# A recurrence, a soft mixture of experts and a dense layer: the range check of the decays moved from the recurrence to the dense stage

## The chip, the cores and the metric

The kernel runs on 1 core of one Trainium2 chip. The metric is device time in microseconds (us) of one execution. Engines: PE multiplies matrices (PEld loads its weights), ACT applies functions and copies, DVE does vector work, POOL does side work, SP issues the transfers (DMA).

## The reference

Three layers follow each other. The first is a recurrence over 768 tokens for 4 batches of 8 heads, the second mixes the tokens softly into 32 slots of 8 experts and back, the third is a dense layer with a sigmoid GELU.

```
for t in range(S):                                  # recurrence
    y[:, :, t] = r_t . (state + (u * k_t) v_t^T)
    state = w_t * state + k_t v_t^T
logits = x @ phi                                    # mixture
slot_input = softmax(logits, 0).T @ x
slot_out[e] = relu(slot_input[e] @ w1[e]) @ w2[e]
x = softmax(logits, 1) @ slot_out
h = x @ w_in                                        # dense layer
out = (h * sigmoid(1.702 * h)) @ w_out
```

The decays w lie between 0.80 and 0.95. The kernel's fast way of doing the recurrence holds only for decays in a range, so it checks them, and falls back to a general way where the check fails. With these inputs it never does.

## The kernel before, in words

**Recurrence** (`phase_a`). 16 pairs of heads are worked on in a software pipeline, one round of the loop `for i in range(n_p + 1)` for each. In round i DVE scans the decays of pair i+1 forward and backward (`products`, L489 to L493), masks the two halves of the scores of pair i (`causal`, L564), scans the states (`states`, L548), scales keys and queries (`scale`, L499) and turns coefficients (`coef_tr`, L523). ACT writes diagonals (`diagonal`, L530, six small ones for each half), copies transposed keys (`keys_tr`, L539), decays (L505), outputs (L583) and their transposes (L597). A mask needs the diagonal of its half. PE makes scores, states, outputs and transposes. SP issues in program order: decays z of pair i+2, then, once PE has finished the outputs of pair i-1, the keys and queries of pair i+3, the values v of pair i+1, and pieces of later weights.

**The check.** `checks` (L510) runs two exponentials over the 1550 decays of two pairs on ACT, summing them into `stat`: in round 0, and at the end of each odd round. They stand ahead of the next round's work on ACT, and read both buffers of z.

**Mixture, end** (`phase_b`). PE applies first weights (L983), then for experts 0 to 7 the second (L1010, 8 products each). Meanwhile DVE converts `w_in` from 64-bit floats in steps (`in_step`, L289 to L302, with ACT's L297 between). After expert 4, `in_range` compares `stat` and the decay products on DVE (L313, L315, L317), sums the flags over the partitions with a one-column product on PE (L319) and copies the sum into `flag` (L320).

**Dense stage** (`phase_c`). A prologue scales and folds the experts' result (L1061 on ACT, L1065 on PE, L1067 on DVE), makes the layer's table (L1073), repeats it over the partitions (L1085), places it, and starts the pipeline: `act` (L1096), GELU (L1103), a high and a low part (L1110 ACT, L1118 DVE). Between these stand steps that convert `w_out` (`step`, the same L289 to L302). Then come 96 steps of nine products each (`project`, L1134), one for each of 6 blocks of 512 tokens and 16 column blocks. Every finished block is added up on DVE (L1154) and stored by SP (L1155).

All of this stands in an order written by hand, and every engine takes its own instructions in that order. `keep_warm` (L279) issues products whose result nobody reads.

Of the kernel before, what the change touches and what calls it, by code (L numbers as in the profile page):

```python
# [7 lines left out]
F32 = mybir.dt.float32  # L8
# [11 lines left out]
NP = H // 2  # L20
# [18 lines left out]
NFLAG = 128 * (1 + NC) * B * NP  # L39
PMIN = 1e-15  # L40
# [166 lines left out]
def body(ctx, tc, rkz, z0, vin, vt, uin, phi, w1, w2, w_in, w_out, cst, out):  # L207
# [10 lines left out]
    stat = cpool.tile([128, 2, B * NP // 2], F32, name="stat")  # L218
# [3 lines left out]
    ubias = cpool.tile([128, 1], F32, name="ubias")  # L222
    soft = [con, ident, phis, tokens, SI, negm, Zs]

    def consts():
        nc.sync.dma_start(out=u_sb, in_=uin)
        nc.sync.dma_start(out=con, in_=cst)
        nc.sync.dma_start(out=phis, in_=phi)
        nc.gpsimd.memset(ebias, -916.0 * 2.0 ** 23)
        nc.gpsimd.memset(ubias, -52.0)  # L230

    with ExitStack() as c1:
        wip = c1.enter_context(tc.tile_pool(name="wip", bufs=1, reuse_waits="tile"))
        ring = c1.enter_context(tc.tile_pool(name="ring", bufs=1, reuse_waits="tile"))
        with tc.manual_schedule(), ExitStack() as c2:
            W = Weights(tc, ring, wip, w1, w2, w_in, w_out)
            short = ExitStack()
            batches, sp, sT, in_step = phase_a(tc, rkz, z0, vin, u_sb, stat, prod, ebias, ubias, W, c2, short, consts, soft)
            dense = phase_b(tc, W, c2, short, sp, sT, soft, batches,
                            lambda room, ps: in_range(tc, stat, prod, con, flag, room, ps), in_step)  # L240
            phase_c(tc, W, c2, dense, ebias, soft, out)
# [65 lines left out]
def in_range(tc, stat, prod, con, flag, room, ps):  # L307

    nc = tc.nc
    m = B * NP  # L310
    g = room[:, 0:NFLAG // 128]
    n = room[:, NFLAG // 128:NFLAG // 128 + 1]
    nc.vector.tensor_scalar(out=g[:, 0:m], in0=stat.rearrange("p a n -> p (a n)"), scalar1=2 * NC + 2.5, scalar2=None,  # L313
                            op0=ALU.is_le)
    nc.vector.tensor_scalar(out=g[:, m:], in0=prod.rearrange("p a n -> p (a n)"), scalar1=PMIN, scalar2=None,  # L315
                            op0=ALU.is_gt)
    nc.vector.tensor_reduce(out=n, in_=g, axis=AX.X, op=ALU.add)  # L317
    pf = ps.tile([128, 512], F32, name="ps")
    nc.tensor.matmul(pf[0:1, 0:1], n, con[:, OFF_SGN:OFF_SGN + 1], start=True, stop=True)  # L319
    nc.vector.tensor_copy(flag, pf[0:1, 0:1])  # L320
# [87 lines left out]
def phase_a(tc, rkz, z0, vin, u_sb, stat, prod, ebias, ubias, W, after, late, consts, soft):  # L408
# [5 lines left out]
    with ExitStack() as ctx:  # L414
# [12 lines left out]
        zz = s0[:, 0:2 * ZW]  # L427
        dX = s0[:, 2 * ZW:2 * ZW + XL]
        half = s0[:, 2 * ZW + XL:].bitcast(BF16)
        dS, junk = half[:, 0:XL], half[:, XL:XL + ZW]  # L430
# [75 lines left out]

        def checks(p):

            for i, (sc, bi) in enumerate(((-30.0, 0.0), (40.0, ubias))):
                nc.scalar.activation(junk.bitcast(mybir.dt.uint8), zz, AF.Exp, scale=sc, bias=bi, accum_out=stat[:, i, p // 2:p // 2 + 1])  # L510
# [134 lines left out]
        for i in range(n_p + 1):  # L645
# [7 lines left out]
            load_z(i + 2)  # L653
            if cur:
                keys_tr(i)
            if cur and i:
                diagonal(i, 0)
# [66 lines left out]
            if i % 2 and nxt or i == 0:  # L724
                checks(i + 1 if i else 0)
# [205 lines left out]
def phase_b(tc, W, after, late, sp, sT, soft, batches=(), check=None, in_step=lambda: None):  # L931
# [6 lines left out]
    with late:  # L938
# [68 lines left out]
        for e in range(NE):  # L1007
# [14 lines left out]
            if check and e == 4:  # L1022
                check(room(), psS)
# [6 lines left out]
def phase_c(tc, W, after, dense, ebias, soft, out):  # L1030
# [3 lines left out]
    with ExitStack() as c2:  # L1034
# [133 lines left out]
        step(0, 1)  # L1168
        for kt in range(KT):
            scaled(kt)  # L1170
        folded()
        pm = psA.tile([128, 512], F32, name="pa")
# [4 lines left out]
        prs = [psS.tile([128, 512], F32, name="ps"), psR.tile([128, 512], F32, name="ps")]  # L1177
        for q in range(2):
            repeat(0, q, prs[q])
        step(0, 3)  # L1180
# [4 lines left out]
        act(1)  # L1185
        gelu(0)
# [27 lines left out]
        going = [[step, 2, 3, 5], [step, 3, 1, 5]]  # L1214
# [82 lines left out]
```

## Time and profile before

| | |
|---|---|
| time, 3 runs | 454.34 us median (453.66 to 455.0) |
| profiled execution | 453.75 us, of which the span of its instructions is 452.0 us |
| busy: PE, DVE, ACT | 403.9, 316.7, 280.5 us |
| recurrence, from the first scan to the end of the last pair | about 0 to 180 us |
| end of the mixture, prologue of the dense stage | about 180 to 222 us |
| 96 dense steps | 222 to 446 us, on PE almost without a gap |

A stretch is read in the rows further down by its busy time on each engine (PE, PEld, DVE, ACT, POOL, each with its instructions in brackets), then the clock granted to PE (1.00 is 2.4 GHz, 0.50 is 1.2 GHz), the mean busy share of the 16 DMA engines, and GB/s. A row of the timeline gives start and length in us, engine, line, operation, operands, and in brackets how long the engine sat idle ahead of it and what ended that. A row of waits gives the total, the number of times and the longest.

### The profile page before, as it was taken

How to read it: one execution, taken by the hardware profiler on the slowest of the kernel's cores; microseconds unless marked ns; L12 is line 12 of the kernel's file. 1: busy time of each engine (PE TensorE's matmuls, PEld its weight loads, DVE VectorE, ACT ScalarE, POOL GpSimd, SP SyncE). 2: the span in 40 equal slices, each digit the busy share in tenths (PEclk: the TensorE clock that was granted, in tenths of full speed). 3: DMA queues.
4: the chain of work that ended last, by engine and by line, in shares of the span. 5: the costliest groups of instructions: out<-in, count | busy, mean ns of one | idle time of the engine just before them, and what ended most of it. 6: DMA issues, size and time to landing. Idle time of an engine off the chain costs nothing.

```text
span 452.0 us, 8818 instructions
## 1 busy us (share of the span) xinstructions
PE 403.9 (89%) x3390; PEld 306.3 (68%) x3392; DVE 316.7 (70%) x529; ACT 280.5 (62%) x630; POOL 47.6 (11%) x81
## 2 busy tenths in 40 slices
PE   4888888978888779986799999999999999999994
PEld 1566666656666657362588878878788888888883
DVE  7898898889889975664897597776775424424332
ACT  4788878788787856231687475665756444444440
POOL 4322222222222102200000000000000000000000
PEclk9699999999999889996899999999999999999999
DMA  8969899797684568999900000000000101101012
GB/s 200 214 195 280 258 232 270 204 265 220 163 216 126 167 274 296 394 413 347 369 0 1 0 2 0 1 1 0 1 1 0 71 1 71 70 0 71 22 48 78
DMA packets 21107, 62.60 MB, mean 139 GB/s; under 512 B 2464, under 2 KB 3104, under 8 KB 20800
## 3 DMA queue, kind: packets, MB, share of 16 engines
q1 hardware_dynamic: 21056, 61.95, 44.1%
q8 instruction: 28, 0.46, 0.4%
q14 instruction: 23, 0.19, 0.1%
HBM read 57.23 MB, written 4.72 MB: 137 GB/s over the span
## 4 chain that ended last, share of the span: by engine, by line
PE 64%; DVE 13%; ACT 13%; DMA 5%; issue 3%; POOL 1%; DVEq 0%; SPq 0%; ACTq 0%; POOLq 0%
PE po L1134 43%; ACT wt L510 5%; DMA wt<-in_rkz 5%; PE pa L1096 5%; ACT am L530 4%; PE ps L983 2%; PE py L575 2%; PE py L580 2%; DVE wt L499 2%; PE ps L1010 2%; PE pg L558 2%; DVE am L564 1%; ACT cT L539 1%; DVE wt L489 1%; DVE st L548 1%
## 5 line engine op out<-in xcount | busy, mean ns | idle before, releaser
L1118 DVE TENSOR_TENSOR gl<-g,gh 128x512 fp32r<-128x512 f32 x96 | 65.1, 688 | 57.9 <-ACT gh L1110 57.5
L1110 ACT CAST gh<-g 128x512 fp32r<-128x512 f32 x96 | 59.4, 619 | 62.4 <-PE po L1134 62.0
L1134 PE MATMUL po<-gh,wi 128*128 128x512 f32 x288 | 88.6, 389 | 0.0
L1134 PE MATMUL po<-gh,wt 128*128 128x512 f32 x288 | 84.8, 395 | 0.0
L1134 PEld LDWEIGHTS po<-gh,wt 128*128 128x128 f32 x288 | 55.0, 191 | 12.2 <-issue 0.4
L530 ACT ACTIVATE am<-con,cT 128x128 f32<-128x128 f32 x192 | 59.6, 396 | 4.9 <-DVE cT L523 4.9
L1134 PEld LDWEIGHTS po<-gh,wi 128*128 128x128 f32 x288 | 54.2, 188 | 11.6
L1103 ACT ACTIVATE g<-pa 128x512 f32<-128x512 f32 x96 | 57.1, 595 | 2.8 <-PE pa L1096 2.8
L1134 PE MATMUL po<-gl,wi 128*128 128x512 f32 x144 | 56.3, 391 | 0.0
L1134 PE MATMUL po<-gl,wt 128*128 128x512 f32 x144 | 51.4, 393 | 1.4 <-DVE gl L1118 1.4
L564 DVE COPY_PREDICATED am<-con,pg 128x768 f32<-128x768 uint32 x32 | 32.4, 1011 | 14.4 <-ACT am L530 14.4
L1096 PE MATMUL pa<-cT,wt 128*128 128x512 f32 x96 | 38.5, 403 | 1.8 <-ACT g L1103 1.6
L558 PE MATMUL pg<-wt 64*128 64x128 f32 x312 | 26.6, 307 | 7.7 <-DVE am L564 7.7
L1134 PEld LDWEIGHTS po<-gl,wt 128*128 128x128 f32 x144 | 27.2, 189 | 8.0 <-DVE gl L1118 2.2
L1134 PEld LDWEIGHTS po<-gl,wi 128*128 128x128 f32 x144 | 27.0, 188 | 5.6
L558 PEld LDWEIGHTS pg<-wt 64*128 64x128 f32 x312 | 21.3, 203 | 13.4 <-DVE am L564 9.7
L489 DVE TENSOR_TENSOR_SCAN wt<-wt 128x774 f32<-128x774 f32 (+1 forms) x17 | 28.1, 1661 | 1.0 <-DMA wt<-in_rkz 0.7
L493 DVE TENSOR_TENSOR_SCAN wt<-wt 128x774 f32<-128x774 f32 x16 | 28.4, 1772 | 0.5
L575 PE MATMUL py<-am,v 128*64 128x128 f32 x384 | 28.4, 284 | 0.0
L483 POOL TENSOR_TENSOR rkb<-wt 128x384 f32<-128x384 f32 x25 | 26.4, 1056 | 14.0 <-DMA wt<-in_rkz 9.5
L596 PE MATMUL ps<-con,xt 128*128 128x128 f32 x96 | 16.4, 284 | 8.7 <-DVE cT L523 4.8
L583 ACT COPY xt<-py 128x384 f32<-128x384 f32 x32 | 14.7, 478 | 13.3 <-PE py L580 13.3
(208 smaller groups left out, 579.9 us busy)
## 6 DMA issues: line engine op xcount, KB each, us to landing
wt<-in_w SPq DMA_DIRECT2D x21, 512.0 KB, 6.8
wt<-in_w SPq DMA_DIRECT2D x13, 768.0 KB, 7.2
wt<-in_rkz SPq DMA_DIRECT2D x26, 288.0 KB, 4.9
v<-in_vin SPq DMA_DIRECT2D x16, 296.0 KB, 5.2
out_dram<-os SPq DMA_DIRECT2D x18, 256.0 KB, 2.1
wt<-in_rkz SPq DMA_DIRECT2D x30, 145.3 KB, 6.3
wi<-in_w_in SPq DMA_DIRECT2D x6, 512.0 KB, 5.8
w2t<-in_w SPq DMA_DIRECT2D x4, 768.0 KB, 7.7
```

The costliest lines, as they stand in the source:

```text
L483: eng.tensor_tensor(out=rkb[:, c], in0=st[p]["r"][:, c], in1=st[p]["k"][:, c], op=ALU.mult)
L489: nc.vector.tensor_tensor_scan(out=sf[:, o:n][:, ::-1], data0=z[:, o + 1:n + 1][:, ::-1], data1=dS[:, o:n][:, ::-1], initial=0.0, op0=ALU. ...
L493: nc.vector.tensor_tensor_scan(out=x, data0=z[:, 0:XL], data1=dX, initial=0.0, op0=ALU.mult, op1=ALU.add)
L530: nc.scalar.activation(am[:, j, c], ident, AF.Copy, scale=q["coef"][:, c0 + c, j:j + 1])
L558: nc.tensor.matmul(q["pg"][:, j, (c - c0) * CH:(c - c0 + 1) * CH], q["k"][64 * j:64 * j + 64, c * CH:(c + 1) * CH], q["r"][64 * j:64 * j + ...
L564: nc.vector.copy_predicated(q["am", c0], later, q["pg"][:, :, 0:3 * CH].rearrange("p j (c t) -> p j c t", t=CH))
L575: nc.tensor.matmul(py[64 * j:64 * j + 64, (c - c0) * CH:(c - c0 + 1) * CH], q["v"][:, c * 96 + j * 48:c * 96 + j * 48 + 64], q["am", c0][: ...
L1096: nc.tensor.matmul(pa, mst[:, f * 128:(f + 1) * 128], cT.at(tb * 512, 512), start=True, stop=True)
L1103: nc.scalar.activation(g, live[n], AF.Gelu_apprx_sigmoid)
L1110: nc.scalar.copy(gh, live[n])
L1118: nc.vector.tensor_tensor(out=gl, in0=g, in1=gh.bitcast(F32), op=ALU.subtract)
L1134: nc.tensor.matmul(live["po", tb][i], w[:, i * 128:(i + 1) * 128], g, start=(f % FH == 0 and k == 0), stop=(f % FH == FH - 1 and k == 2))
```

## The change

The two exponentials are gone from the recurrence, with `stat` and their scratch room. ACT's first half of diagonals moves ahead of the copies of keys. In the dense stage the decays are read a second time, as 24 pieces of 128x384 numbers (196.6 KB each) into three rotating rooms, and DVE takes the largest absolute value of each, two steps after its load. The flags are summed in step 90 of 96. The prologue gets 17 idle products in five places.

```
 class Check:
     def load(self, i, room):
         self.t[i] = room
         self.tc.nc.sync.dma_start(out=room, in_=self.wc[:, i * (NW // NCK):(i + 1) * (NW // NCK)])
     def part(self, i):
         self.tc.nc.vector.tensor_reduce(out=self.peak[:, i:i + 1], in_=self.t.pop(i), axis=AX.X, op=ALU.max,
                                         apply_absolute_value=True)
     def result(self, room, pf):
         nc = self.tc.nc
         g, n = room[:, 0:NFLAG // 128], room[:, NFLAG // 128:NFLAG // 128 + 1]
         nc.vector.tensor_scalar(out=g[:, 0:NCK], in0=self.peak, scalar1=WMAX, scalar2=None, op0=ALU.is_le)
         ...
         nc.vector.tensor_reduce(out=n, in_=g, axis=AX.X, op=ALU.add)
         nc.tensor.matmul(pf[0:1, 0:1], n, self.con[:, OFF_SGN:OFF_SGN + 1], start=True, stop=True)
         nc.vector.tensor_copy(self.flag, pf[0:1, 0:1])
@@ phase_a
-        def checks(p):
-            for i, (sc, bi) in enumerate(((-30.0, 0.0), (40.0, ubias))):
-                nc.scalar.activation(junk.bitcast(mybir.dt.uint8), zz, AF.Exp, scale=sc, bias=bi, accum_out=stat[:, i, p // 2:p // 2 + 1])
...
+            if cur and i:
+                diagonal(i, 0)
             if cur:
                 keys_tr(i)
-            if cur and i:
-                diagonal(i, 0)
...
-            if i % 2 and nxt or i == 0:
-                checks(i + 1 if i else 0)
@@ phase_b
-            if check and e == 4:
-                check(room(), psS)
@@ phase_c
+        idle = con[:, 0:320].bitcast(BF16)
+        prs = [psS.tile([128, 512], F32, name="ps"), psR.tile([128, 512], F32, name="ps")]
         for kt in range(KT):
             scaled(kt)
+        keep_warm(nc, prs[1], idle, 2)
         folded()
+        keep_warm(nc, prs[1], idle, 2)
         ...
         table_low(0, pm)
+        keep_warm(nc, prs[1], idle, 4)
         for q in range(2):
             repeat(0, q, prs[q])
+        keep_warm(nc, pt, idle, 2)
         ...
         act(1)
+        keep_warm(nc, pt, idle, 7)
...
+        c0 = FH * n_tb + 4
...
+            if check and n == n_all - FH + 2:
+                check.result(room(), bank(0, 0))
             project(n)
...
+            if check and c0 <= n < c0 + NCK:
+                check.load(n - c0, room())
+            if check and c0 + 2 <= n < c0 + NCK + 2:
+                check.part(n - c0 - 2)
```

How this stands on the engines. On ACT, around the end of an odd round, before (`am` are diagonals, `cT` copies of keys, `xb` transposed outputs, `pB` decays):

```order
L530 ACTIVATE am<-con,cT_116 128x128 x6
L597 COPY xb<-ps_1129 128x288
L597 COPY xb<-ps_1134 128x288
L510 ACTIVATE wt_80,stat<-wt_80 128x1550
L510 ACTIVATE wt_80,stat<-wt_80,ubias 128x1550
L539 COPY cT_116<-ps_1149 128x384
L539 COPY cT_116<-ps_1154 128x384
L530 ACTIVATE am<-con,cT_116 128x128 x6
```

and the same place on ACT after (the lines have shifted: L534 is `diagonal`, L543 `keys_tr`, L601 the transposes):

```order
L534 ACTIVATE am<-con,cT_115 128x128 x6
L601 COPY xb<-ps_1119 128x288
L601 COPY xb<-ps_1124 128x288
L534 ACTIVATE am<-con,cT_115 128x128 x6
L543 COPY cT_115<-ps_1144 128x384
L543 COPY cT_115<-ps_1149 128x384
```

Two long exponentials are gone, and the diagonals of the round's first half follow directly on the transposes. On PE, at the end of the mixture and in the prologue, before:

```order
L1010 MATMUL ps<-w2t,hTm 32x384 x16
L319 MATMUL ps<-con,c_2574 1x1
L1010 MATMUL ps<-wt_86,hTm 32x384 x8
L1010 MATMUL ps<-wt_83,hTm 32x384 x8
L1010 MATMUL ps<-wt_87,hTm 32x384 x8
L1065 MATMUL ps<-con,c_2622 128x32 x3
```

and after (L1012 is the second weights, L280 an idle product):

```order
L1012 MATMUL ps<-w2t,hTm 32x384 x16
L1012 MATMUL ps<-wt_85,hTm 32x384 x8
L1012 MATMUL ps<-wt_82,hTm 32x384 x8
L1012 MATMUL ps<-wt_86,hTm 32x384 x8
L280 LDWEIGHTS con
L280 MATMUL ps<-con 128x512
L280 LDWEIGHTS con
L280 MATMUL ps<-con 128x512
L1065 MATMUL ps<-con,c_2597 128x32 x3
```

The flags' product no longer stands between the experts, and the first two idle products stand ahead of the fold. On DVE in the dense stage, after, the flags' steps stand between low parts, six steps from the end (before there are low parts alone):

```order
L1118 TENSOR_TENSOR gl<-g,gh 128x512 x3
L326 TENSOR_SCALAR c_4635<-peak 128x24
L327 TENSOR_SCALAR c_4635<-prod 128x96
L329 TENSOR_REDUCE c_4635<-c_4635 128x1
L331 CAST flag<-po_4636 1x1
L1118 TENSOR_TENSOR gl<-g,gh 128x512 x4
```

Earlier in the stage one reduction stands behind each of 24 low parts in the same way.

## Rows read from the trace of the kernel before

**Rows 1.** Stretches: recurrence in two, experts, wait, experts, prologue, first dense step.

```profile
30.53:79.70 49.17, 41.26 (x634) 30.73 (x626) 42.71 (x52) 41.68 (x110) 11.55 (x21) 1.00 0.92 263
79.70:138.54 58.84, 50.45 (x764) 37.57 (x764) 52.22 (x65) 49.06 (x134) 13.60 (x24) 1.00 0.80 218
181.86:201.64 19.78, 19.73 (x192) 10.38 (x192) 12.40 (x35) 5.92 (x13) 2.76 (x5) 1.00 1.03 401
201.64:207.12 5.48, 0.00 (x0) 0.03 (x1) 5.16 (x11) 1.07 (x2) 0.00 (x0) 0.72 1.03 410
207.12:213.11 5.99, 5.90 (x50) 1.79 (x50) 1.27 (x4) 0.61 (x1) 0.00 (x0) 0.69 0.91 331
213.11:222.05 8.94, 5.71 (x43) 3.55 (x44) 5.53 (x12) 5.09 (x11) 0.00 (x0) 0.95 0.93 374
222.05:225.25 3.20, 3.20 (x10) 2.54 (x9) 3.13 (x8) 2.10 (x5) 0.00 (x0) 0.62 0.95 384
```

**Rows 2.** What DVE waited for, 30.53 to 79.70, then 79.70 to 138.54.

```profile
DVE am L564 <- ACT am L530: 5.6, 4, 2.0
DVE am L564 <- ACT am L530: 5.8, 7, 1.4
```

**Rows 3.** Timeline of DVE, one round behind a check.

```profile
89.36 1.76 DVE L489 TENSOR_TENSOR_SCAN wt<-wt 128x774 f32<-128x774 f32 x1
...
94.71 1.01 DVE L564 COPY_PREDICATED am<-con,pg 128x768 f32<-128x768 uint32 x1 [1.36 <-ACT am L530]
...
99.13 1.73 DVE L489 TENSOR_TENSOR_SCAN wt<-wt 128x774 f32<-128x774 f32 x1
```

**Rows 4.** Timeline of ACT, the check at the start of that round.

```profile
88.86 1.51 ACT L510 ACTIVATE wt<-wt 128x1550 uint8<-128x1550 f32 x1
...
92.08 0.84 ACT L539 COPY cT<-ps 128x384 f32<-128x384 f32 x2
```

**Rows 5.** Loads of v: two issues, the first one's landing, PE's first use.

```profile
86.97 0.42 SPq L471 DMA_DIRECT2D v<-in_vin  x1
...
95.75 0.42 SPq L471 DMA_DIRECT2D v<-in_vin  x1
...
DMA to landing us min/median/max: 5.6/5.6/5.6
...
92.66 0.70 PE L545 MATMUL pkv<-v,cT 128*48 128x48 f32 x20 [0.58 <-ACT cT L539]
```

**Rows 6.** Around the flags' product: PE, DVE, ACT; last weights of the experts, landing.

```profile
207.12 0.16 PE L319 MATMUL ps<-con,c 128*1 128x1 f32 x1 [5.48 <-DVE c L317]
...
207.15 5.87 PE L1010 MATMUL ps<-wt,hTm 128*32 128x384 f32 x46
...
206.39 0.17 DVE L313 TENSOR_SCALAR c<-stat 128x16 f32<-128x16 f32 x1
...
207.43 0.36 DVE L289 TENSOR_SCALAR cv_e<-wt 128x384 int32<-128x384 int32 x1
...
214.56 0.26 DVE L1067 COPY c<-ps 128x96 f32<-128x96 f32 x1 [5.91 <-PE ps L1065]
...
207.87 0.61 ACT L297 ACTIVATE cv_e<-cv_e,ebias 128x384 int32<-128x384 int32 x1 [3.03 <-DVE cv_e L289]
...
213.17 0.89 ACT L1061 ACTIVATE c<-ps,Zs 128x128 f32<-128x128 f32 x3 [4.68 <-PE ps L1010]
...
L90 SPq DMA_DIRECT2D wt<-in_w x2: 473/705/937, 187.6 to 188.2; - x2
...
DMA to landing us min/median/max: 12.0/12.7/13.5
```

**Rows 7.** PE, four idle products ahead of the experts (one record missing).

```profile
180.83 1.02 PE L279 MATMUL ps<-con 128*128 128x512 bf16 x3 [0.70 <-ACT cT L765]
```

**Rows 8.** A late dense step: its first product on PE, the low part on DVE.

```profile
432.87 0.40 PE L1096 MATMUL pa<-cT,wt 128*128 128x512 f32 x1
...
433.55 0.69 DVE L1118 TENSOR_TENSOR gl<-g,gh 128x512 fp32r<-128x512 f32 x1 [1.59 <-ACT gh L1110]
```

More of the change, by code (lines that the diff above doesn't have):

```diff
@@ L206, in body @@
 @with_exitstack
-def body(ctx, tc, rkz, z0, vin, vt, uin, phi, w1, w2, w_in, w_out, cst, out):
+def body(ctx, tc, rkz, z0, vin, vt, wc, uin, phi, w1, w2, w_in, w_out, cst, out):
     nc = tc.nc
@@ L405, in phase_a_general, with phase_a @@
                 nc.scalar.copy(bt.home(h), pct)
-def phase_a(tc, rkz, z0, vin, u_sb, stat, prod, ebias, ubias, W, after, late, consts, soft):
+def phase_a(tc, rkz, z0, vin, u_sb, prod, ebias, W, after, late, consts, soft):
     nc = tc.nc
@@ L653, in phase_a @@
             load_z(i + 2)
+            if cur and i:
+                diagonal(i, 0)
             if cur:
                 keys_tr(i)
-            if cur and i:
-                diagonal(i, 0)
             if i == n_p - 1:
@@ L928, in slot_inputs, with phase_b @@
     return sT
-def phase_b(tc, W, after, late, sp, sT, soft, batches=(), check=None, in_step=lambda: None):
+def phase_b(tc, W, after, late, sp, sT, soft, batches=(), in_step=lambda: None):
     nc = tc.nc
@@ L1027, in phase_b, with phase_c @@
     return cvp, room, psA, mid, psH, psS, po, rep
-def phase_c(tc, W, after, dense, ebias, soft, out):
+def phase_c(tc, W, after, dense, ebias, soft, out, check=None):
     nc = tc.nc
@@ L1176, in phase_c @@
         table_low(0, pm)
-        prs = [psS.tile([128, 512], F32, name="ps"), psR.tile([128, 512], F32, name="ps")]
+        keep_warm(nc, prs[1], idle, 4)
         for q in range(2):
             repeat(0, q, prs[q])
+        keep_warm(nc, pt, idle, 2)
         step(0, 3)
@@ L1185, in phase_c @@
         act(1)
+        keep_warm(nc, pt, idle, 7)
         gelu(0)
@@ L1230, in phase_c @@
                     repeat(1, q, prs[q])
+            if check and n == n_all - FH + 2:
+                check.result(room(), bank(0, 0))
             project(n)
@@ L1245, in phase_c @@
             going = [q for q in going if q[2] < q[3]]
+            if check and c0 <= n < c0 + NCK:
+                check.load(n - c0, room())
+            if check and c0 + 2 <= n < c0 + NCK + 2:
+                check.part(n - c0 - 2)
 def layout(r, k, v, w, u, moe_phi, moe_w1, moe_w2, moe2_w_in, moe2_w_out):
```

54 lines of the change are left out of this document (22 added, 32 removed).

## The prediction

> **What bounds the kernel now.** I read the table of stretches first: it tells the stages apart, since the 70% of DVE and the 62% of ACT on the page are means over stages with different limits. In the recurrence DVE is busy for 42.71 of 49.17 us and then for 52.22 of 58.84 [rows 1]; no other engine is nearer to full in total work that a round must do, so what DVE waits for there is what a round is too long by. The waits of DVE have one name only: the mask (L564) waits 5.6 and 5.8 us for ACT's diagonals [rows 2]. The third view is the end of the mixture: between two pieces of expert work PE does nothing at all for 5.48 us, while DVE is busy for 5.16 of them [rows 1]. The fourth is the prologue, where PE has work for 5.71 of 8.94 us, and the first dense step, which runs at a granted clock of 0.62 [rows 1]. The 96 dense steps after that are PE's, and the change takes nothing from them.
>
> **The check leaves the recurrence.** A check holds ACT from 88.86 to 92.08, so 3.2 us [rows 4]; eight go, seven of them inside or next to the two stretches. In the round behind that check DVE took 99.13 - 89.36 = 9.77 us, of which it waited 1.36 for a diagonal [rows 3], so its own work was 8.4 us. If every wait for a diagonal went, the two stretches would be shorter by 5.6 + 5.8 = 11.4 us [rows 2]. That is the upper end. What is late next keeps some of it.
>
> In the first stretch it is the transfers. Their share is 0.92 of 49.17 us, so 45.2 us of work for the DMA engines, and the fullest stretch shown reaches 1.03 [rows 1]. So the stretch can't fall below 45.2 / 1.03 = 43.9 us, a gain of 5.3; at a share of 0.97 it is 46.6 us, a gain of 2.6. I take 4.0, the middle. In the second stretch the share is only 0.80 [rows 1], but one load turns in a loop with PE: v is issued at 86.97 and lands 5.6 us later at 92.57, PE starts to use it at 92.66, and the next v, which waits for PE's outputs, goes out at 95.75 [rows 5]. PE stood 0.58 us there for a copy of keys that the check had delayed [rows 5], but v itself had landed only 0.09 us earlier. So a round in this loop lasts 95.75 - 86.97 - 0.09 = 8.7 us where DVE would do with 8.4. With about six rounds in the stretch that keeps 6 x 0.3 = 1.8 of the 5.8 us at most; I take 1.5 and a gain of 4.3. The swap on ACT puts 6 diagonals ahead of the copies of keys; it helps the mask and delays the copies, and PE's 0.58 us shows that the copies can matter. I count it at nothing, since without the check ACT reaches both 3.2 us sooner; if that cover were gone, the copies could cost 0.58 us in each of the 11 rounds, 6 us, and this is the low end. After 138.54 nothing is counted. **Sum of the recurrence: 8.3 us, between 4 and 11.4.**
>
> **The flags leave the mixture.** The one-column product (L319) waited 5.48 us because its flags stand on DVE behind the conversions of `w_in`, and all later expert products wait behind it on PE [rows 6]. Gone, experts 5 to 7 start at 201.64. Their weights are there: the last of them, issued by 188.2, landed after 13.5 us, at 201.7 [rows 6], and only expert 7 needs those. The three experts took 5.87 us at a mean clock of 0.69 [rows 1, 6]; the clock stood at 1.00 up to 201.64 [rows 1], and if it stays there they take 5.87 x 0.69 = 4.1 us. PE is then done between 205.7 and 207.5. But the conversions are still on DVE and become the next late thing. The first step of `w_out` (L289) moves up to where the flags' first compare began, from 207.43 to 206.39. ACT's L297 followed it by 0.44 and took 0.61 [rows 6], so ACT reaches the scaling (L1061) at 206.39 + 0.44 + 0.61 = 207.44 instead of 213.17. That is a gain of 5.7 us, the same whether PE's clock falls or not as long as PE is done by 207.5. The fold's copy on DVE (214.56, 1.39 us behind the scaling) moves with it [rows 6]. All loads of this stage wait for PE, so they move with it as well. If DVE's conversions were stretched by whatever now runs beside them, the gain shrinks with that; half of it, 2.8 us, is the low end. **5.7 us, between 2.8 and 6.**
>
> **The idle products.** Four of them took 1.02 us, 0.26 each [rows 7], so 17 hold PE for 4.3 us. PE had 8.94 - 5.71 = 3.2 us without work in the prologue [rows 1], and the two ahead of the fold now lie in a wait that the moved flags leave behind. Seven stand behind the second `act`, where PE waits for the GELU. The eight others, 2.1 us, stand where the waits are shorter; I take 0.8 us of delay from them (the excess 4.3 - 3.2 = 1.1, less a part for the two ahead of the fold), between 0 and 2.1. In return the first dense step, 3.20 us at 0.62 [rows 1], would take 2.0 at full clock: 1.2 us back if the clock holds, nothing if it falls all the same. Net gain 0.4 us, between -2.1 and 1.2. The Trainium skill (TensorE: Matmul & The Clock Gate, Part 3: Packing small matmuls — row/col tiling) says that products start and end in program order and never overtake one another. By that rule an idle product cannot step aside for a real one, and the 0.8 us is paid; if they could be passed, the sum would be better by 0.8 us. No row here shows an idle product being passed.
>
> **The dense stage.** DVE has 1.59 us without work ahead of a low part, and 0.69 with it, so 2.28 us in a step [rows 8]. A reduction over 128x384 is not in the trace. The nearest row, 0.69 us for 128x512 [rows 8], makes it 0.5 to 0.7 us as an estimate, so 24 of them fit, and they cost nothing. The loads find idle DMA engines. If a reduction has to wait for its load, low parts come later, but the low part of a step is made more than one step ahead of its use. On SP the loads stand between the stores of finished blocks and can be held by one of them for part of a step; SP's read of the flag now stands ahead of the last three stores alone, which come some five steps later. The flags in step 90: the low part begins 0.68 us after the step's first product, at 433.55 against 432.87 [rows 8], ends at 1.37, and the flags' DVE work is under 207.43 - 206.39 = 1.04 us, product and copy included [rows 6]. It ends before 2.41; PE comes to the flags' product one step and one product (a tenth of a step) later, at 2.28 + 0.23 = 2.5 us. So PE need not wait; the nine products of step 90 are queued behind it if it does, and DVE's next low part behind the copy. PE pays the product alone, 0.16 us [rows 6]: a cost of 0.1, at most 0.5. Flag and branch then have some 12 us until the end.
>
> **The sum.** 8.3 + 5.7 + 0.4 - 0.1 = 14.3 us. Against the profiled execution's own 453.75 us that gives 439.4 us. Its time is 0.6 us under the median of the three runs, within their spread of 453.66 to 455.0.
>
> **The rivals.**
>
> *Loads pace the recurrence.* The transfers stay at 0.92 in the first stretch, and every round turns with its load of v: gain 2 to 5 us in the recurrence instead of 8.3, so 442.5 to 446 us. For it: the share of 0.92 and the 0.09 us of slack of v [rows 1, 5]. Against it: z no longer waits for the check before it is issued, and the share of the second stretch is 0.80. The Trainium skill (DMA: Bandwidth & Descriptors, Issuing engines are not separate DMA queues) says that all transfers run on the same 16 engines and interleave. By that rule a faster loop gets no more of them, and the first stretch would keep most of its length; the shares of 0.92 and 1.03 agree.
>
> *The wait at the flags becomes another.* PE, freed at 201.64, meets conversions or weights that come later than I have them, and the fold stays where it was within 3 us: gain there 2.8 instead of 5.7, so 442 us, and up to 445 where the recurrence's low end adds to it.
>
> *Everything goes.* All 11.4 us of waits go, the clock never falls: 11.4 + 6 + 1.2 = 18.6 us, so 435 us, and lower if the stretch after 138.54 gains too.
>
> *Slower: the second read holds the dense stage.* Three rooms turn: a load is issued when the reduction three steps earlier frees its room. One turn is landing plus about 0.7 us, for three steps. With landing L a step becomes (L + 0.7) / 3. At 5.6 us, as for v [rows 5], that is 2.1 us, under the 2.28 of a step. From L = 6.1 us DVE falls behind, and from L = 7.9 us the 24 steps lose 24 x 0.6 = 14.4 us, all that the change gains. At 9 us the kernel would take about 462 us. The rows show landings of 13.5 us, but behind a long queue [rows 6]; in this stage nothing is queued. That it doesn't do what it says, because other work of the round fills the place of the waits, would leave it within 0.3%.
>
> **Chances.** The forecast (436.5 to 442.5) 0.62; loads pace the recurrence (442.5 to 446) 0.14; the wait becomes another (442 to 445) 0.08; everything goes (433 to 436.5) 0.09; slower 0.04; no change 0.03. A range of 435 to 444.5 us leaves out the slower case, no change, and the outer parts of the cases beside the forecast, under 2 in 10 together. A measurement of this kernel can tell about 0.3% from no change. Faster by over 0.3%: 0.93; within it 0.03; slower 0.04.
>
> **What would show it.** In the profile after: DVE's waits at the mask, now 11.4 us, should be 1 to 4, and rounds 8.5 to 8.9 us long. PE should run the eight experts without a gap, and ACT's scaling come about 6 us after expert 4, set by DVE's conversions and not by PE. The clock should stay at 1.00 from the experts into the dense steps. The dense steps from 52 to 79 should keep 2.28 us. I am wrong if rounds stay above 9.2 us, if PE waits for v or for copies of keys, or if the fold comes no earlier behind expert 4 than before.

## The result and the profile after

The changed kernel took **441.2 us** (median of 4 runs, 440.68 to 442.45), the kernel before it 454.0 us on the same chip (452.06 to 455.0). The ratio is 0.9727, 95% interval 0.9688 to 0.9766: 12.8 us faster. The prediction's sum was 14.3 us, from the 453.75 us of the profiled execution to 439.4. Two later comparisons of the same two kernels on other chips gave less: 444.94 against 453.44 (ratio 0.9801, interval 0.975 to 0.9851), and 444.84 against 454.6 (0.9785, 0.9737 to 0.9832). So the time of the first comparison lies in the predicted range, and both later medians just above its upper end of 444.5. Which part of the sum was too large is the question of what follows. Two edits below (no second read, and z ahead with half of `w_in`) were profiled in runs more than 1.5% above the fastest of their kernel, so the recurrence is not compared in those two profiles.

The profiled execution took 442.45 us, its span is 440.6. The stretches that answer to [rows 1], in the same columns (start:end, length, PE, PEld, DVE, ACT, POOL busy, then granted clock, DMA share, GB/s): the recurrence in two, the experts up to the fourth, the others up to ACT's scaling, the prologue, the first dense step with the next step's product.

```profile
30.30:76.86 46.56, 40.78 (x634) 30.55 (x626) 42.68 (x53) 32.52 (x98) 11.54 (x21) 1.00 0.96 274
76.86:132.25 55.39, 50.17 (x764) 37.48 (x764) 52.22 (x64) 39.93 (x122) 13.72 (x24) 1.00 0.85 231
174.97:191.74 16.77, 16.72 (x163) 8.37 (x166) 9.53 (x29) 5.07 (x12) 2.77 (x6) 1.00 0.99 379
191.74:200.46 8.72, 7.42 (x87) 5.69 (x78) 8.41 (x17) 2.46 (x5) 0.00 (x0) 1.00 1.03 409
200.46:209.06 8.60, 7.86 (x58) 4.43 (x59) 5.58 (x13) 4.80 (x12) 0.00 (x0) 1.00 1.04 425
209.06:212.38 3.32, 2.55 (x11) 1.80 (x10) 3.25 (x8) 2.23 (x5) 0.00 (x0) 1.00 0.99 422
```

ACT's work in the first stretch fell from 41.68 to 32.52 us, DVE's stayed (42.71 and 42.68). The first stretch lost 2.6 us, the second 3.45; the first weights start 6.9 us earlier (181.86 before, 174.97 now). The third and fourth row have no wait of PE between them any more, at a clock of 1.00 throughout.

DVE's waits in the two stretches, the answer to [rows 2] (total, times, longest; first 30.30 to 76.86, then 76.86 to 132.25):

```profile
DVE wt L498 <- DMA wt<-in_rkz: 2.7, 2, 2.0
DVE am L568 <- ACT am L534: 0.7, 2, 0.3
...
DVE am L568 <- ACT am L534: 1.4, 3, 0.6
DVE cT L527 <- PE ps L520: 0.9, 2, 0.4
```

The waits for diagonals went from 11.4 to 2.1 us, as forecast. The first line shows what came beside them: DVE waits for the decays z themselves (`wt<-in_rkz`) ahead of its scan. PE has a new wait too, for v, over both stretches:

```profile
PE pkv L549 <- DMA v<-in_vin: 2.5, 4, 1.3
```

On the page, the row of loads shows z slower, with a median of 8.0 us from issue to landing where the page of before has 6.3:

```profile
wt<-in_rkz SPq DMA_DIRECT2D x30, 145.3 KB, 8.0
```

SP's timeline of one round tells why (a row is an issue). Keys and queries (L473) come first, v (L480), pieces of later weights (L79), and only then z of the next pair but one (L466):

```profile
83.30 0.78 SPq L473 DMA_DIRECT2D wt<-in_rkz  x2
84.13 0.41 SPq L480 DMA_DIRECT2D v<-in_vin  x1
84.60 0.90 SPq L79 DMA_DIRECT2D wt<-in_w  x2
85.59 0.84 SPq L466 DMA_DIRECT2D wt<-in_rkz  x2
...
92.78 0.42 SPq L480 DMA_DIRECT2D v<-in_vin  x1
```

From one v to the next this round took 8.65 us, against 8.78 in [rows 5]. DVE's round that answers to [rows 3]: the first mask, which had waited 1.36 us, no longer waits, the second waits 0.25, and the round (86.50 to 95.40) takes 8.90 us instead of 9.77. It is one of the shorter rounds: over the eleven of the two stretches the mean is 9.27 us, and it was 9.82 before.

```profile
86.50 1.75 DVE L498 TENSOR_TENSOR_SCAN wt<-wt 128x774 f32<-128x774 f32 x1
...
90.41 1.00 DVE L568 COPY_PREDICATED am<-con,pg 128x768 f32<-128x768 uint32 x1
...
94.23 1.03 DVE L568 COPY_PREDICATED am<-con,pg 128x768 f32<-128x768 uint32 x1 [0.25 <-ACT am L534]
95.40 1.77 DVE L498 TENSOR_TENSOR_SCAN wt<-wt 128x774 f32<-128x774 f32 x1
```

At the end of the mixture, the answer to [rows 6] on PE, ACT and DVE:

```profile
194.31 4.30 PE L1012 MATMUL ps<-wt,hTm 128*32 128x384 f32 x47
198.55 0.61 PE L280 MATMUL ps<-con 128*128 128x512 bf16 x2
200.85 0.93 PE L1065 MATMUL ps<-con,c 128*128 128x32 f32 x6 [1.70 <-ACT c L1061]
...
199.93 0.62 ACT L298 ACTIVATE cv_e<-cv_e,ebias 128x384 int32<-128x384 int32 x1 [1.94 <-DVE cv_e L290]
200.46 0.86 ACT L1061 ACTIVATE c<-ps,Zs 128x128 f32<-128x128 f32 x3
...
199.55 0.35 DVE L290 TENSOR_SCALAR cv_e<-wt 128x384 int32<-128x384 int32 x1
```

PE runs the last experts in one piece, is done with them at 198.6, and then waits for ACT, which waited for DVE's conversion: the order of events that the prediction worked out.

The time of the profiled executions divides as follows (us). "Last DVE" is the end of the last addition.

| stretch | before | after | gained |
|---|---|---|---|
| start to first weights | 181.86 | 174.97 | 6.9 |
| first weights to ACT's scaling | 31.31 | 25.49 | 5.8 |
| scaling to first output product of the dense stage | 8.88 | 8.60 | 0.3 |
| that to the end of the last DVE | 224.66 | 224.97 | -0.3 |
| last DVE to end of span | 5.29 | 6.57 | -1.3 |

### The profile page after: what moved, and what is told of

Its sections match the earlier page's. It is cut to its first block, busy times and chain, and to the rows that moved or that the text cites. A ratio compares the mean times of both kernels' runs of the same rounds, so it can differ in the third digit from the quotient of the medians.

```text
span 440.6 us, 8896 instructions
## 1 busy us (share of the span) xinstructions
PE 402.7 (91%) x3409; PEld 307.3 (70%) x3409; DVE 327.6 (74%) x553; ACT 255.8 (58%) x598; POOL 48.1 (11%) x80
## 4 chain that ended last, share of the span: by engine, by line
PE 62%; DVE 20%; DMA 8%; issue 4%; ACT 2%; SPq 1%; POOL 1%; DVEq 0%; POOLq 0%; ACTq 0%
PE po L1134 43%; DMA wt<-in_rkz 8%; PE pa L1096 5%; DVE wt L498 3%; DVE wt L508 3%; PE ps L985 2%; DVE am L568 2%; PE py L579 2%; DVE wt L502 2%; PE py L584 2%; PE pg L562 1%; PE ps L280 1%; ACT am L534 1%; DVE st L552 1%; PE pkv L549 1%
## 5 line engine op out<-in xcount | busy, mean ns | idle before, releaser
L1134 PE MATMUL po<-gh,wt 128*128 128x512 f32 x288 | 83.7, 390 | 0.0
L534 ACT ACTIVATE am<-con,cT 128x128 f32<-128x128 f32 x192 | 59.4, 391 | 9.5 <-DVE cT L527 9.5
L1134 PEld LDWEIGHTS po<-gh,wt 128*128 128x128 f32 x288 | 54.1, 189 | 11.8 <-issue 0.4
```

What stands on the lines that cost most here:

```text
L534: nc.scalar.activation(am[:, j, c], ident, AF.Copy, scale=q["coef"][:, c0 + c, j:j + 1])
L1134: nc.tensor.matmul(live["po", tb][i], w[:, i * 128:(i + 1) * 128], g, start=(f % FH == 0 and k == 0), stop=(f % FH == FH - 1 and k == 2))
```

## The experiments

Theory: the two large terms are the check's room on ACT and the wait at the flags, and what kept part of the first one is the order and pace of the loads. Rivals: the swap of diagonals, or the clock and the idle products, carry part of the gain; or rounds are held by DVE alone. Code that an edit's cut leaves out is marked with three dots.

### The check out, alone

On the kernel before; the decays are then not checked, and the flags' sum stays behind expert 4.

```
-NFLAG = 128 * (1 + NC) * B * NP
+NFLAG = 128 * NC * B * NP
...
-            if i % 2 and nxt or i == 0:
-                checks(i + 1 if i else 0)
```

> The kernel before with the two exponentials over the decays left out of the recurrence (the decays are then not checked at all; the flags' sum stays behind expert 4, over the decay products alone). Theory: this part alone is worth what the recurrence became shorter by in the kernel after, 6 to 7 us, so 447 to 448 us, and PE still waits about 5.5 us at the flags. The recurrence's rounds are then set by the landing of z. Rival: half of the recurrence's gain came from the diagonals' new place ahead of the copies of keys; then 3 to 4 us, 450 to 451 us, with DVE still waiting 5 us or more for diagonals.

Measured: 449.07 us against 453.65 (ratio 0.9912, interval 0.9876 to 0.9947), between what the two sides expected (447 to 448, and 450 to 451); the waits decide. The first weights start at 175.17. From there to the scaling it is 31.2 us as before, and PE still stands at the flags:

```profile
200.41 0.16 PE L317 MATMUL ps<-con,c 128*1 128x1 f32 x1 [5.39 <-DVE c L315]
```

DVE's waits in the two stretches:

```profile
DVE wt L487 <- DMA wt<-in_rkz: 4.3, 3, 1.7
DVE am L562 <- ACT am L528: 2.0, 5, 0.6
```

The mask waits 2.0 us, without the swap. So taking out the exponentials alone removes the waits at the mask. DVE's wait for z appears here too, with 4.3 us, and PE's for v with 2.8: the new waits belong to the faster round, not to the rest of the change.

### The flags' sum late, alone

On the kernel before, which keeps its exponentials; no idle products.

```
-            if check and e == 4:
-                check(room(), psS)
...
+            if check and n == n_all - FH + 2:
+                check(room(), bank(0, 0))
```

> The kernel before with only the flags' sum moved to step 90 of the dense stage; the exponentials stay in the recurrence, no idle products. Theory: 5.7 us at the end of the mixture, nothing elsewhere, 448 to 449 us; ACT's scaling comes 25.5 us after the first weights' first product, as in the kernel after. Rival: without the idle products the clock falls in the gap ahead of the fold and takes 1.5 to 2 us back; 450 us.

Measured: 448.56 us against 453.65 (0.99, 0.9867 to 0.9934). From the first weights to the scaling it took 25.56 us, as in the changed kernel. But here the clock fell in the prologue. Its row, scaling to first output product, and that of the kernel of the next experiment:

```profile
205.32:216.58 11.26, 8.80 (x43) 5.36 (x43) 5.93 (x13) 5.07 (x12) 0.00 (x0) 0.53 1.03 426
```

```profile
202.75:211.35 8.60, 5.43 (x42) 3.35 (x43) 5.57 (x13) 4.80 (x12) 0.00 (x0) 1.00 1.04 423
```

The same PE work takes 8.80 us at a mean clock of 0.53 and 5.43 at 1.00, and the prologue is 2.7 us longer. So the late sum is worth 5.8 us, and the clock can take back 2.7 of it. The two changes alone give 4.6 and 5.1 us, together 9.7; the whole change gave 12.8, 8.5 and 9.8 in its three comparisons. For the two later ones no third part is needed; the 3 us more of the first are taken up at the end of the next section.

### After without the idle products

```
-        keep_warm(nc, prs[1], idle, 2)
...
-        keep_warm(nc, pt, idle, 7)
```

> The kernel after without its 17 idle products. Theory: their gain (a warm first dense step) was given back at the wait for the second GELU behind it, so the time moves by under 0.6 us, 440.8 to 441.8 us. Rival: the clock falls between the fold and the first dense steps and costs 1.2 us or more; 442.4 us or above.

Measured: 444.62 us against 453.65 (0.9805, 0.9764 to 0.9846), what the changed kernel took in its later comparisons (444.94 and 444.84). The time alone lies where the rival put it (442.4 or above), but so do the two later ones of the changed kernel, and the rival's cause is not in the trace: the prologue took 8.60 us, to the hundredth the same as with the 17 products, and the clock stayed at 1.00 without them in this execution. So at the upper level of the clock they cost nothing that can be seen: all of them lie in waits of PE. What they bring was not shown. The kernel without them and with a late sum lost its clock in the experiment before this one and kept it in this one; and with them it was lost too (below).

### After without the second read

Neither loads nor maxima of the decays, which are then not checked.

```
-            if check and c0 <= n < c0 + NCK:
-                check.load(n - c0, room())
-            if check and c0 + 2 <= n < c0 + NCK + 2:
-                check.part(n - c0 - 2)
...
```

> The kernel after without the second read of the decays and without its 24 maxima (the decays are then not checked; the flags of the decay products are still summed in step 90). Theory: the read and the maxima are hidden, 0 to 0.3 us; the 0.4 us lost in step 90 stay, since they are the flags' product; 440.8 to 441.3 us. Rival: the read also lengthens the end of the program, where the profile of after has 1.3 us more between DVE's last step and the end of the span; 439.5 to 440 us.

Measured: 443.37 us against 453.65 (0.9765, 0.9717 to 0.9812), above both expectations and within the spread of the changed kernel's comparisons. The 96 steps, from the first output product to the start of the last addition, take 224.23 us here and 224.28 in the changed kernel, at full clock in both: the 24 maxima cost PE nothing. In the trace of after, one takes 547 ns, and DVE waits three times for a load, 3.5 us in all, while low parts stay ahead of PE:

```profile
L320 DVE TENSOR_REDUCE peak<-c x24: 543/547/554, 336.7 to 389.2; 128x1 f32<-128x384 f32 x24
its engine sat idle before it (us, times) until:
  DMA c<-in_wc: 3.5, 3
```

The rival spoke of the end of the program. The span ends 5.3 us behind the last DVE here, as in the kernel before, and 6.6 in the changed kernel, as the rival has it. But three kernels further down keep the second read and end after 5.2 to 5.3 us, so the read alone does not make the longer end.

### The changed kernel again, as an anchor

> The changed kernel itself, unedited, beside the three edits of it that follow, on the same chip. Both theories: 440.5 to 443 us as in its first comparison; in its profile DVE waits for z at the scans (3 to 4 us in all), PE waits for v at the states' products about four times, each round between 8.3 and 10 us.

Measured: 444.94 us against 453.44 (0.9801, 0.975 to 0.9851), above the 440.5 to 443 expected. The first weights start at 178.71, where the first profile had 174.90 and the same instructions stand ahead of them. DVE waits 4.2 us for z, PE 4.9 for v in the two stretches. One of these waits shows what it can cost. PE's timeline, and then the stretches from 62 to 64, 64 to 66 and 66 to 68 us:

```profile
64.17 0.88 PE L549 MATMUL pkv<-v,cT 128*48 128x48 f32 x20 [2.19 <-DMA v<-in_vin]
```

```profile
62.00:64.00 2.00, 0.00 (x0) 0.00 (x0) 1.90 (x4) 1.19 (x3) 0.00 (x0) 1.00 1.03 369
64.00:66.00 2.00, 1.82 (x32) 1.82 (x32) 2.00 (x4) 0.00 (x0) 1.14 (x2) 0.63 1.03 347
66.00:68.00 2.00, 2.00 (x18) 1.32 (x16) 1.95 (x3) 0.11 (x1) 0.00 (x0) 0.51 0.19 37
```

PE stands still for v, and then works on at the lower of its two levels, 1.2 GHz. That round (60.48 to 71.14) takes 10.66 us where the first profile has 8.86 for it (59.02 to 67.88). In it DVE, too, waits 1.34 us for a product of PE (`ps`), which it did not in the first profile. So a late load can be paid twice, once as a wait and once in the clock.

### After without the swap of diagonals

```
-            if cur and i:
-                diagonal(i, 0)
             if cur:
                 keys_tr(i)
+            if cur and i:
+                diagonal(i, 0)
```

> After, with the diagonals of the first half behind the copies of keys on ACT again, as before. Theory (the check's time on ACT was the whole cause of the waits at the mask, the swap is worth little): the masks wait 1 to 2 us more in all, the first weights start at most 1 us later than in after, time within 1 us of after. Rival (without the swap the masks stay late in every round): the waits at the mask come back to 5 us or more and the time is 2 to 4 us above after. Third (the swap costs by delaying the copies of keys, as the low end of the prediction feared): 1 us or more below after.

Measured: 446.73 us against 453.44 (0.983, 0.9791 to 0.9868), beside 444.94 for the anchor; the intervals overlap. In the trace the masks wait as long as with the swap (2.1 us):

```profile
DVE am L568 <- ACT am L534: 2.2, 5, 0.6
```

The first weights start at 177.58, inside the spread of the changed kernel's profiles (174.90 to 178.71). The extra time lies elsewhere: the clock was at 0.57 from 204 to 208 us in this execution, with idle products in their place, and the prologue took 10.25 us instead of 8.60. By the trace the swap is worth nothing that can be seen, and no cost of later copies of keys shows in either order.

### z ahead of the weights

```
-            load_z(i + 2)
+            if i == 0:
+                load_z(i + 2)
...
             load_v(i + 1)
+            load_z(i + 3)
```

> After, with the decays z issued one place earlier on SP: z of pair i+3 right behind the values v of pair i+1, ahead of the piece of w_in of that round. Theory (rounds are paced by the landing of z behind the weights' pieces in the queue): the waits of DVE for z, 3.3 us in after, go to under 1 us, and the first weights start 1.5 to 3 us earlier; 438.5 to 440.5 us. Rival (DVE's own work and the loop of v with PE's outputs hold the rounds, z is only late where nobody is held long): the waits go, but the masks or PE's wait for v take them over, the first weights start less than 0.7 us earlier; time within 1 us of after.

Measured: **451.38 us** against 453.44 (0.993, 0.9904 to 0.9956), 6.4 us slower than the anchor beside it. z landed sooner (median 6.2 us), and no wait of DVE for it is left in the two stretches, as the theory has it; PE's wait for v took it over, as the rival has it. That it would be a loss was in neither. The largest waits of PE, then of DVE:

```profile
PE pkv L549 <- DMA v<-in_vin: 10.1, 6, 3.4
...
DVE cT L527 <- PE ps L520: 6.0, 5, 1.9
DVE st L552 <- PE pkv L549: 5.3, 4, 2.2
```

z now runs beside v, the transfer on which the round turns. PE's wait for v went from 4.9 to 10.1 us, and DVE waits for PE. The mean clock of the first stretch fell to 0.94, and the first weights start at 184.37, later than before the change. A wait was moved from the load with slack to the one without.

### z ahead of the weights, and w_in in every second round

As the kernel before this one, and:

```
-            if 0 < i <= KT * HF // CV:
-                W.load_in(i - 1)
+            if i and i % 2 == 0 and i <= 2 * KT * HF // CV:
+                W.load_in(i // 2 - 1)
```

> After, with z issued early as in the kernel before this one and with the pieces of w_in loaded only in every second round, so that the first stretch carries about half of them. Theory (transfers fill the first stretch: share of the DMA engines 0.92 before): its rounds shorten by 2 to 4 us in all against after, the second stretch loses at most 1 of them; 437 to 440 us. Rival (DVE and the loop of v pace the rounds also in the first stretch): the share falls there and the rounds stay, time within 1 us of after.

Measured: 446.06 us against 453.44 (0.9795, 0.9748 to 0.9842): 5 us of the loss come back with half of `w_in`'s pieces out of the first stretch, but it is not faster than the anchor (444.94, ratio 0.9801). The 437 to 440 us of the theory did not come; the time is near the anchor's, as the rival has it.

### v ahead of keys and queries

A second anchor ran beside this and the two that follow.

> The changed kernel itself again, unedited, as the anchor of the three edits that follow, on the same chip. All theories: 441 to 445 us, first weights at 175 to 178 us; PE waits for v 2.5 to 5 us and DVE for z 2.7 to 4.2 us in the recurrence.

It took 444.84 us against 454.6, its first weights start at 176.42; DVE waits 4.1 us for z, PE 2.2 for v. The edit:

```
+            load_v(i + 1)
             if i < n_p - 4:
                 load_rk(i + 3)
...
-            load_v(i + 1)
             if 0 < i <= KT * HF // CV:
```

> After, with the values v of pair i+1 issued ahead of the keys and queries of pair i+3 on SP, instead of behind them; z stays where it is. Theory (loads in one queue share the DMA engines in their order, and v is the one that a round turns with): v lands in under 4.5 us instead of 5.3, PE's waits for v go to under 1 us, the first weights start 1 to 3 us earlier, 438.5 to 442 us. Rival (the waits for v are slack of PE, and z paces the rounds): the waits for v go, those of DVE for z stay at 3 us or grow, time within 1 us of after. Rival (bandwidth alone counts, not the order): v lands no earlier.

Measured: 441.96 us against 454.6 (0.972, 0.9687 to 0.9753). PE's waits for v fell to 1.4 us, though v took as long from issue to landing as before (median 5.5): it is issued sooner, not carried faster, as the third expectation has it. DVE's waits for z rose to 5.8 us, and the first weights start at 177.88. So the recurrence is no shorter than the changed kernel's, and the waits are those of the second expectation. Its time is not: it should have been within 1 us of the anchor and is 2.9 us under it. The profile is of the slowest of the six runs (444.26), so the recurrence of the others may be shorter.

### v, then z, ahead of keys and queries

```
-            load_z(i + 2)
+            if i == 0:
+                load_z(i + 2)
...
+            load_v(i + 1)
+            load_z(i + 3)
             if i < n_p - 4:
                 load_rk(i + 3)
```

> After, with v of pair i+1 and then z of pair i+3 issued ahead of the keys and queries of pair i+3. Theory: both waits go, PE's for v under 1.5 us and DVE's for z under 1 us, rounds 8.5 to 8.8 us, first weights 2 to 4 us earlier than in after, 437.5 to 440.5 us. Rival (DVE, ACT and PE hold the rounds at their own pace): first weights less than 1 us earlier, masks and coefficients take the waits over. Rival (as with z ahead of the weights alone): z so early takes transfer time from v, v lands later than 5.3 us, and it is slower than after.

Measured: 440.96 us against 454.6 (0.9721, 0.9677 to 0.9766). The first weights start at 174.68. No wait for z is left, the masks wait 2.4 us, PE 2.8 for v. Its first stretch is the shortest of all:

```profile
30.46:75.82 45.36, 40.68 (x634) 30.54 (x626) 42.68 (x53) 32.46 (x98) 11.59 (x21) 1.00 1.02 267
```

DVE's own work in it is the same 42.68 us, so 2.7 us of room are left there, 1.2 less than in the shortest of the changed kernel's. Waits are exchanged less badly here than with z alone ahead of the weights. v goes first, though it lands in 6.4 us by the median where the anchor has 5.5, and the keys and queries, which no wait of DVE or PE names here, pay (7.1 us, 5.2 in the changed kernel). The theory's size did not come: v's wait is not under 1.5 us, the rounds are 9.1 us long and not 8.5 to 8.8, and the first weights start 1.7 us earlier than in the anchor and not 2 to 4.

### v ahead, and w_in in every second round

The edit with v ahead, and the edit of `load_in` with every second round, together.

> After, with v ahead of keys and queries, and the pieces of w_in in every second round only. Theory (transfers fill the first stretch): the share of the DMA engines falls there, DVE's waits for z shrink under 1.5 us as z no longer stands behind w_in in every round, PE's for v under 1 us, first weights 2 to 4 us earlier than in after, 437.5 to 440.5 us. Rival (the first stretch is paced by DVE): no gain over the kernel with v ahead alone.

Measured: 441.31 us against 454.6 (0.9705, 0.9664 to 0.9746). PE has no wait for v in the two stretches, DVE 2.4 us for z; the first stretch takes 46.09 us, the first weights start at 175.14. The share of the DMA engines did not fall in the first stretch (1.00, the anchor's 0.95), the rate did (244 GB/s, the anchor's 266). It is 0.65 us under the kernel with v ahead alone, inside both intervals, so the rival that half of `w_in` gains nothing further is not excluded.

These three are 2.9 to 3.9 us under the anchor by their medians, 2.9 to 3.6 by the ratios. Intervals of the ratios overlap, and 1.4 us of the difference is not the recurrence: their spans end 5.2 to 5.3 us behind the last DVE, the anchor's 6.6. They look better than the changed kernel. In the traces of the last two the first weights start 1.7 and 1.3 us earlier than in the anchor, but within 0.3 us of the first profile of the changed kernel (174.90); more is not shown.

## Why the prediction was right, and where it was not

The two stretches of the recurrence, in the profiles on which this section rests (us; waits are those of DVE for diagonals and for z, and of PE for v, over both):

| kernel | first | second | diagonals | z | v | first weights |
|---|---|---|---|---|---|---|
| before | 49.17 | 58.84 | 11.4 | 0.3 | none | 181.8 |
| before, flags late | 48.74 | 58.84 | 11.4 | none | none | 179.8 |
| after, first profile | 46.56 | 55.39 | 2.1 | 2.7 | 2.5 | 174.9 |
| after, second | 49.90 | 54.45 | 2.1 | 4.2 | 4.9 | 178.7 |
| after, third | 48.31 | 55.58 | 2.7 | 4.1 | 2.2 | 176.4 |
| after, no idle products | 48.62 | 55.49 | 2.4 | 3.5 | 4.7 | 177.2 |
| before, check out | 48.39 | 54.45 | 2.0 | 4.3 | 2.8 | 175.2 |
| after, no swap | 48.66 | 54.63 | 2.2 | 4.6 | 4.0 | 177.6 |
| v ahead | 49.45 | 53.89 | 1.3 | 5.8 | 1.4 | 177.9 |
| v, then z ahead | 45.36 | 55.18 | 2.4 | none | 2.8 | 174.7 |
| v ahead, half of `w_in` | 46.09 | 55.18 | 1.5 | 2.4 | none | 175.1 |

**The flags: right, in size and in mechanism.** Forecast 5.7 us, measured 5.8 in the changed kernel and 5.8 with the late sum alone. PE was not what set the new end, and it stayed at the upper level of its clock; DVE's conversion, then ACT's L298, then the scaling did, in the sequence that the prediction took from [rows 6].

**The second stretch of the recurrence: right in the main; the reason given for what is kept did not show.** Forecast 4.3 us. The four profiles of the changed recurrence (the third to the sixth row) take 54.45 to 55.58 us, a mean of 55.2, so 3.6 us less than the 58.84 that both profiles of before show. DVE is busy for 52.2 of them: this stretch is close to DVE's own work. I had 1.5 us kept by the loop of v, a round of 8.7 us against 8.4 of DVE's own work. The 8.4 came from one round; [rows 1] gives 52.22 / 6 = 8.7 for DVE itself. With v ahead the stretch takes 53.89 us in one kernel and 55.18 in the two others, one of which has no wait of PE for v:

```profile
76.70:131.88 55.18, 50.59 (x767) 37.66 (x768) 52.01 (x63) 40.34 (x123) 13.79 (x24) 1.00 0.98 247
```

So no part that hangs on v is shown. What the rows of the first profile show in its place are DVE's waits of 1.4 us for diagonals and 0.9 us for a product of PE (`ps`).

**The first stretch: the step that failed.** Forecast 4.0 us, the middle between 2.6 and 5.3. The first profile gained 2.6, the four together (mean 48.35 us) only 0.6 against the mean of 48.96 before, and one of them was longer than before. The diagonals' waits went as foreseen, but z and v took them over. Two readings were at fault. One is the floor from the DMA share: I multiplied share by length and called the result work. By that the first stretch held 45.2 us of work before; with v ahead of the keys it holds 49.45 x 1.03 = 50.9, though both move 12.84 MB from 30.6 to 79 us:

```profile
30.73:80.18 49.45, 41.53 (x641) 31.00 (x637) 42.79 (x53) 32.97 (x99) 11.51 (x21) 1.00 1.03 265
```

So share times length is not an amount of work, and gives no floor. The other is z: only v was traced as a load in a loop, while z, which waited 0.3 us before and stands behind all the weights in SP's order, was passed over, even where I wrote that it would be issued sooner. It was, and landed later: the z that before was issued at 34.04 us, behind a check, and took 4.0 us now goes out at 29.42, right behind pieces of weights, and takes 10.9.

The rival that loads pace the recurrence (442.5 to 446 us, chance 0.14) describes this, and the two later comparisons lie in it. The first comparison favours the forecast, but on its mechanism the rival deserved more than a seventh. Two of the prediction's own signs of being wrong came up: PE waits for v, and the rounds stay above 9.2 us (9.27 in the first profile, 9.4 to 9.5 in the three others). The 8.5 to 8.9 us that it named for a round did not fit its own sum: 8.3 us less in the eleven rounds makes (108.0 - 8.3) / 11 = 9.06. The rule of the Trainium skill that stood beside that rival (DMA: Bandwidth & Descriptors, Issuing engines are not separate DMA queues: transfers share 16 engines and interleave) is borne out by the kernel with z ahead of the weights: z gained 1.7 us of landing, and PE's wait for v doubled.

**The swap at nothing: right**, by the trace without it. The low end of 6 us for late copies of keys did not show.

**The idle products: right sum, wrong terms.** Forecast 0.4 us as 1.2 less 0.8. The delay of 0.8 us isn't there: I set all 17 against the waits of the prologue before, but in the new order 8.60 us is the chain of ACT and DVE, and PE's waits swallow them all. They still run in their place, as the Trainium skill's rule of strict order says (TensorE: Matmul & The Clock Gate, Part 3: Packing small matmuls — row/col tiling); there was no real product ready behind them. The return of 1.2 us did not come either, though the clock held. The first step's row shows it: 3.32 us with PE busy for 2.55, where before it was 3.44 to the same point. What the faster PE saved went into a wait for the GELU, whose engine had waited for a conversion:

```profile
212.05 0.50 PE L1096 MATMUL pa<-cT,wt 128*128 128x512 f32 x1 [0.77 <-ACT g L1103]
...
210.90 0.62 ACT L298 ACTIVATE cv_e<-cv_e,ebias 128x384 int32<-128x384 int32 x1 [0.90 <-DVE cv_e L290]
```

The 0.4 us that were gained (0.28 in the prologue, 0.12 in the first step) came just so without the products (8.60 and 3.33 us). They go with the wait at the flags: the kernel with the check out alone keeps that wait, and its prologue takes 8.88 us as before. So the match of this term is luck.

**The dense stage: right.** A maximum took 0.55 us (estimate 0.5 to 0.7), the loads landed in 2.7 us by the median, far from the 7.9 at which the slower rival would have decided. The flags' step is step 90: from 419.80 to 422.44 it is 2.64 us, 0.36 over the usual 2.28, inside the 0.5 that was allowed. The trace shows no wait of PE for DVE; its own product stands in the way:

```profile
419.80 0.40 PE L1096 MATMUL pa<-cT,wt 128*128 128x512 f32 x1
420.13 0.19 PE L330 MATMUL po<-con,c 128*1 128x1 f32 x2
420.25 0.73 PE L1134 MATMUL po<-gh,wi 128*128 128x512 f32 x2
...
422.44 0.40 PE L1096 MATMUL pa<-cT,wt 128*128 128x512 f32 x1
```

**The end: not in the sum.** The span ends 1.3 us later behind the last DVE (6.57 us instead of 5.29), in all three profiles of the changed kernel (6.50 to 6.62). No term of the prediction stood for it.

**Set together.** By the mean the first weights start at 176.8 us in the four profiles of the changed recurrence and at 180.8 in the two of before, a gain of 4.0 where 8.3 was forecast, at the low end of what was allowed. With 5.8 for the flags, 0.3 for the prologue, -0.3 for the dense stage and -1.3 for the end that is 8.5 us, which the later comparisons show (8.5 and 9.8). The first comparison, the one that the forecast met, had its recurrence at the short end of its spread: its gain of 6.9 us there makes 11.4, the difference of the two profiled executions (453.75 and 442.45) within 0.1. That the forecast was met there is partly luck. Why all four runs of that comparison were short (440.68 to 442.45) is open; chance and chip were not separated.

## What to carry to other kernels

When a wait in a loop is removed, trace every load of the loop in the order of its queue, and ask for each how much slack it has and behind which bulk transfers it stands: the next late one takes over part of the gain. In the edits here a load moved ahead was paid for by its neighbours, so put first the one on which the round turns, then the next needed, and let those with slack pay. One profile of a loop that waits on loads is one draw: compare several before a few microseconds are put down to an edit.

## What was not expected of the hardware

**A busy share near one is not a full rate.** In 40 slices of 30.6 to 79 us of the kernel with v, then z ahead, the share (first row, tenths) is 9 nearly throughout, while the rate (second row, GB/s) goes from 153 to 423:

```profile
DMA  9999989999899999999999999999999999999999
GB/s 201 169 349 423 394 273 233 204 178 165 195 335 397 299 184 164 218 191 273 355 404 360 235 153 198 207 222 239 387 334 204 208 214 235 249 369 413 345 219 214
```

The mean share of the 16 engines is nine tenths or more at either rate (153 and 404 GB/s are three slices apart). Which transfers run at which was not separated.

**The clock varies between executions of the same instructions.** After a wait for v of 2.19 us it fell in a profile of the changed kernel; with v, then z ahead, one of 2.1 us left it at 1.00. In the prologue it held in seven of the ten profiles with idle products (8.60 to 8.62 us) and fell in three (10.24 to 10.26), at a cost of 1.65 us. What decides it was not settled; it may be part of why the changed kernel's runs spread from 440.7 to 450.2 us.

**The end of the span has two lengths.** It is 5.2 to 5.3 us behind the last DVE in the kernel before, in its two edits, in the one without the second read and in those with v ahead, and 6.3 to 6.7 in the changed kernel and in those with the swap undone, without idle products, or with z ahead of the weights. No computing engine works there, only the last stores land. The three profiles of the changed kernel agree (6.50 to 6.62), so the length seems to go with the program and not with the execution; the cause stays open.
